# Rounding weights in 16 pieces, loading the first unit's operands first, and scanning a whole unit at once in a gated-attention and MLP kernel

## The chip, the cores and the metric

The kernel runs on one NeuronCore of a Trainium2 chip. The metric is device time in microseconds for one execution. Runs of the kernel before took 786.53, 787.57 and 788.98 us; the median is 787.57 us. In the text PE is the matmul engine, DVE the vector engine, ACT the scalar engine, POOL GpSimd, and SP the engine whose queue issues most of the DMAs. Each engine works off its own queue in order.

## The reference

A gated linear attention runs over 768 steps for 4 batches of 8 heads, with 48 channels per head; its result, 3072 tokens of 384 channels, goes through a two-layer network with 2048 hidden channels and the activation h - tanh(h).

```python
def _attn_ref(q, k, v, alpha):               # each (4, 8, 768, 48), float32
    ...
    for t in range(S):
        state = alpha[:, :, t, :, None] * state + np.einsum('bhd,bhe->bhde', k[:, :, t], v[:, :, t])
        y[:, :, t] = np.einsum('bhd,bhde->bhe', q[:, :, t], state)
    return y.astype(np.float32)

def _moe_ref(x, w_in, w_out):                # (3072, 384), (384, 2048), (2048, 384)
    h = x @ w_in
    g = h - np.tanh(h)
    return (g @ w_out).astype(np.float32)
```

The two weight matrices arrive as float64. The chip has to turn each of their 1.57 million numbers into float32 before a matmul can use it.

## The kernel before

**Units.** The work is cut into 12 units of 256 tokens, three for each batch; a unit has two chunks of 128 tokens. A unit goes through two generators. `gla(u)` is the attention: it transposes alpha, k and q so that channels lie on partitions (L344), forms running products of alpha over each chunk from the right (`U`, L351) and from the left (written over `aT`, L361), multiplies them onto k and q (POOL, L364 and L365), forms scores (`sc`, L382, masked into `pm`, L385), outputs (`y`, L394 and L398) and the new state (`tp`, `kn`, `up`, L418 to L429). Its result is `xT`; a part of it is moved between partitions by six small DMAs per chunk from `xs` (L411). `moe(u)` is the network, in 8 steps: `first(s)` makes 256 hidden channels `h` (L442) and their activation `g` (ACT L448 to L455, DVE L451 to L453); `second(s)` multiplies `g` by `w_out` into `o` (L462) two steps later. At the end of a unit two ACT copies (L474) and two DMAs write the 256 rows of the output.

**Weights.** `load_weight` (L37 to L66) loads one piece of int64 words and rounds it: on DVE four passes cut out, clamp, shift and sign the exponent (L55, L57, L58, L60) and one cuts out the upper mantissa (L62); ACT turns both parts of the mantissa to float (L63, L64), POOL adds them (L65), and DVE multiplies mantissa and exponent into the weight (L66). There are 12 pieces of 512 columns for `w_in` and 16 of 384 columns for `w_out`, 28 in all.

**Order.** A list `order` gives every step of every generator a due time; it is sorted and the steps are written in that order. All weight pieces are due before the first step of `moe(0)`. A scheduler then places the instructions on each engine from these priorities and its own estimates; the engines' queues are fixed when the program starts. Loads of a unit (`load`, L327 and L332) and of weights (L48) are all issued by SP. The raw tiles of alpha, k and q exist twice, one set for even and one for odd units. After the last unit a flag decides whether a slow general version must recompute everything; with these inputs it isn't run.

Of the kernel before, what the change touches and what calls it, by code (L numbers as in the profile page):

```python
# [8 lines left out]
FP32 = mybir.dt.float32  # L9
# [9 lines left out]
CU = 2  # L19

# [15 lines left out]
def load_weight(nc, pool, dst, rows):  # L36

    V, A, GP = nc.vector, nc.scalar, nc.gpsimd  # L40
    n = dst.shape[-1]
    if rows[0][1].dtype == FP32:
        for at, src in rows:
            nc.sync.dma_start(out=dst[at], in_=src)
        return
    raw = pool.tile([P, 512], I64, name="raw")
    for at, src in rows:
        nc.sync.dma_start(out=raw[at, 0:n], in_=src)  # L48
    words = raw.bitcast(I32).rearrange("p (n w) -> p n w", w=2)
    lo, hi = words[:, 0:n, 0].bitcast(mybir.dt.uint32), words[:, 0:n, 1]  # L50
    e = pool.tile([P, 512], I32, name="e", tag="u")[:, 0:n]
    m = pool.tile([P, 512], I32, name="m", tag="z1")[:, 0:n]
    low = pool.tile([P, 512], FP32, name="low", tag="z2")[:, 0:n]
    man = pool.tile([P, 512], FP32, name="man", tag="w")[:, 0:n]
    V.tensor_scalar(out=e, in0=hi, scalar1=20, scalar2=0x7FF,  # L55
                    op0=ALU.logical_shift_right, op1=ALU.bitwise_and)
    V.tensor_scalar(out=e, in0=e, scalar1=896, scalar2=1151, op0=ALU.max, op1=ALU.min)  # L57
    V.tensor_scalar(out=e, in0=e, scalar1=23, scalar2=0x3FFFFFFF,  # L58
                    op0=ALU.logical_shift_left, op1=ALU.bitwise_and)
    V.scalar_tensor_tensor(out=e, in0=hi, scalar=-0x40000000, in1=e,  # L60
                           op0=ALU.bitwise_and, op1=ALU.bitwise_or)
    V.tensor_single_scalar(out=m, in_=hi, scalar=0xFFFFF, op=ALU.bitwise_and)  # L62
# [189 lines left out]
def fast(tc, q, k, v, alpha, moe_w_in, moe_w_out, out, w_in, w_out, ident, ok, pad_rows):  # L252
# [17 lines left out]
    with ExitStack() as ctx:  # L270
# [19 lines left out]
        raws = [[consts.tile([P, NP, R, D], FP32, name=f"{n}{i}") for n in ("ar", "kr", "qr")]  # L290
                for i in range(2)]
        for i in range(2):
            for t, x in zip(raws[i], (1.0, 0.0, 0.0)):
                GP.memset(t[:, :, R - 1, :], x)

        Us = [consts.tile([P, NP, CU, P], FP32, name=f"U{i}") for i in range(2)]
        for t in Us:
            GP.memset(t[:, :, :, P - 1:P], 1.0)
# [4 lines left out]
        def weights():  # L303

            w = 512
            for i in range(d_ff // w):
                cols = slice(i * w, (i + 1) * w)
                for j in range(KT):
                    load_weight(nc, two, w_in[:, j, cols],
                                [(at, moe_w_in[f0:f0 + at.stop - at.start, cols]) for at, f0 in pad_rows[j]])  # L310
                yield
                for f in range(i * w // P, (i + 1) * w // P):
                    load_weight(nc, two, w_out[:, f, :], [(slice(0, P), w_out_r[:, f, :])])
                yield
# [3 lines left out]
        def load(u):  # L318
            b, i = divmod(u, UPB)
            t0 = i * TU  # L320
            for t, x in zip(raws[u % 2], (alpha, k, q)):
# [9 lines left out]
            for c in range(CU):  # L331
                nc.sync.dma_start(out=vt[:, c], in_=v[b, :, t0 + c * P:t0 + (c + 1) * P, :].rearrange("h p d -> p h d"))  # L332
# [157 lines left out]
        for _, _, what, u in sorted(order):  # L490
            if (what, u) not in live:
                live[what, u] = make[what](u) or iter(())
# [81 lines left out]
```

## Time and profile before

| | us |
|---|---|
| median of the runs | 787.57 |
| the profiled execution, whole | 785.88 |
| its span, first to last instruction | 783.7 |
| PE busy | 627.0 (80% of the span) |
| DVE busy | 477.8 (61%) |
| ACT busy | 336.7 (43%) |
| POOL busy | 118.2 (15%) |

The profile gives for each engine its busy time, for each line of the kernel its instructions with their mean duration, and for each gap what the engine waited for. A slice picture divides the span into 40 parts of 19.6 us; each digit is the busy share of a part in tenths. A windows table gives busy times for stretches that one chooses, and a timeline lists instructions by start time.

### The profile page before, as it was taken

The numbers are of one execution on the slowest core, as the hardware profiler recorded it, in microseconds if no ns is written. First come the engines' busy times: TensorE is split into PE (matmuls) and PEld (weight loads), VectorE is DVE, ScalarE is ACT, GpSimd is POOL, SyncE is SP. The second block draws the span as 40 slices with busy tenths as digits, with TensorE's granted clock in tenths as the row PEclk, the third lists the DMA queues.
The fourth block names the chain that finished last, engine by engine and source line by source line (L and its number), as shares of the span: only waits on it lengthen the run. The fifth ranks groups of instructions, "written<-read, shape, count | busy, mean of one in ns | idle before, by whom it ended". The sixth has DMA issues, their size and how long they took to land. (4 is left out here: it accounts for less than half of the span.)

```text
span 783.7 us, 9136 instructions
## 1 busy us (share of the span) xinstructions
PE 627.0 (80%) x3089; PEld 462.9 (59%) x3089; DVE 477.8 (61%) x828; ACT 336.7 (43%) x725; POOL 118.2 (15%) x110
## 2 busy tenths in 40 slices
PE   0350090008989999989999999999999999999996
PEld 0240070006667677767776767767767777677773
DVE  5357977877858768393685672864728434344332
ACT  1122143235446364454453653544536444454542
POOL 2212332232030203011020120110201200000000
PEclk9999995558999999999999999999999999999999
DMA  9015744366036226244352250130100000000000
GB/s 199 17 53 142 147 105 119 97 164 136 1 86 119 55 62 129 63 98 79 78 113 54 61 126 23 32 69 24 23 20 6 1 23 4 6 18 3 20 1 25
DMA packets 58424, 51.03 MB, mean 65 GB/s; under 512 B 30976, under 2 KB 54784, under 8 KB 58368
## 3 DMA queue, kind: packets, MB, share of 16 engines
q1 hardware_dynamic: 58368, 50.36, 28.4%
q8 instruction: 26, 0.43, 0.2%
q14 instruction: 30, 0.25, 0.1%
HBM read 44.43 MB, written 4.72 MB: 63 GB/s over the span
## 5 line engine op out<-in xcount | busy, mean ns | idle before, releaser
L442 PE MATMUL h<-xT,w_in 128*128 128x256 f32 x1152 | 277.7, 387 | 0.9 <-DVE w L451 0.9
L462 PE MATMUL o<-w_out,g 128*128 128x384 f32 x768 | 259.7, 486 | 3.1 <-DVE g L453 3.1
L442 PEld LDWEIGHTS h<-xT,w_in 128*128 128x128 f32 x1152 | 214.6, 192 | 45.2 <-issue 5.2
L462 PEld LDWEIGHTS o<-w_out,g 128*128 128x128 f32 x768 | 145.8, 190 | 89.8 <-DVE g L453 3.7
L451 DVE TENSOR_TENSOR w<-h,u 128x512 f32<-128x512 f32 x96 | 66.0, 687 | 157.6 <-ACT u L448 157.3
L448 ACT ACTIVATE u<-h 128x512 f32<-128x512 f32 x96 | 57.2, 596 | 162.6 <-PE h L442 162.1
L418 PE MATMUL tp<-ident,kT 128*128 128x128 f32 x80 | 14.1, 305 | 132.2 <-POOL kT L364 131.3
L418 PEld LDWEIGHTS tp<-ident,kT 128*128 128x128 f32 x80 | 10.8, 156 | 136.0 <-POOL kT L364 131.8
L452 DVE SCALAR_TENSOR_TENSOR z<-z,w 128x512 f32<-128x512 f32 x96 | 71.8, 747 | 9.7 <-ACT z L449 2.8
L389 POOL TENSOR_TENSOR state<-state,ends 48x192 f32<-48x192 f32 x40 | 26.6, 666 | 293.5 <-DVE state L429 200.4
L453 DVE SCALAR_TENSOR_TENSOR g<-z,z 128x512 f32<-128x512 f32 x96 | 66.1, 688 | 6.4
L385 DVE TENSOR_TENSOR pm<-sc,mask 128x512 f32<-128x512 f32 x48 | 31.9, 685 | 60.3 <-PE sc L382 60.3
L449 ACT ACTIVATE z<-u 128x512 f32<-128x512 f32 x96 | 60.6, 631 | 2.7
L455 ACT ACTIVATE big<-u 128x512 f32<-128x512 f32 x96 | 59.1, 615 | 0.0
L450 ACT ACTIVATE z<-u 128x512 f32<-128x512 f32 x96 | 59.0, 615 | 0.0
L361 DVE TENSOR_TENSOR_SCAN aT<-aT,inv 128x128 f32<-128x128 f32 x96 | 44.8, 510 | 0.2
L65 POOL TENSOR_TENSOR man<-man,low 128x384 f32<-128x384 f32 (+1 forms) x28 | 31.4, 1123 | 88.1 <-ACT man L63 88.1
L364 POOL TENSOR_TENSOR kT<-kT,U 128x1024 f32<-128x1024 f32 x12 | 28.4, 2370 | 100.1 <-DVE kT L344 100.1
L365 POOL TENSOR_TENSOR qT<-qT,aT 128x1024 f32<-128x1024 f32 x12 | 28.9, 2407 | 94.9 <-DVE qT L344 57.7
L405 ACT COPY xs<-y 48x128 f32<-48x128 f32 x48 | 12.4, 258 | 65.2 <-PE y L398 64.9
L351 DVE TENSOR_TENSOR_SCAN U<-aT 128x127 f32<-128x127 f32 x96 | 34.6, 423 | 4.0 <-POOL kT L364 3.8
L474 ACT COPY ob<-o 128x384 f32<-128x384 f32 x24 | 11.5, 479 | 58.2 <-PE o L462 58.2
(57 smaller groups left out, 517.9 us busy)
## 6 DMA issues: line engine op xcount, KB each, us to landing
raw<-in_moe_w_out_dram SPq DMA_DIRECT2D x16, 384.0 KB, 3.4
vt<-in_v_dram SPq DMA_DIRECT2D x24, 192.0 KB, 3.5
raw<-in_moe_w_in_dram SPq DMA_DIRECT2D x24, 192.0 KB, 3.8
ar<-in_alpha_dram SPq DMA_DIRECT2D x24, 192.0 KB, 4.6
kr<-in_k_dram SPq DMA_DIRECT2D x24, 192.0 KB, 4.6
qr<-in_q_dram SPq DMA_DIRECT2D x24, 192.0 KB, 5.2
out_dram<-ob SPq DMA_DIRECT2D x24, 192.0 KB, 1.9
ar<-in_alpha_dram SPq DMA_DIRECT2D x24, 176.0 KB, 4.6
```

The source lines that it names most:

```text
L351: V.tensor_tensor_scan(out=U[:, g, c, P - 2::-1], data0=aT[:, g, c, P - 1:0:-1], data1=aT[:, g, c, P - 1:0:-1], initial=1.0, op0=ALU.mult, ...
L361: V.tensor_tensor_scan(out=aT[:, g, c, :], data0=aT[:, g, c, :], data1=aT[:, g, c, :], initial=inv[:, g, c:c + 1], op0=ALU.mult, op1=ALU.b ...
L385: V.tensor_mul(pm[hh], sc[hh], mask.unsqueeze(1).to_broadcast([P, NP, P]))
L442: T.matmul(h[:, a, :], lhsT=w_in[:, j, f * P:(f + 1) * P], rhs=x_t[:, j, :], start=(j == 0), stop=(j == KT - 1))
L448: A.activation(sq, h, AF.Square)
L449: A.activation(z1, sq, AF.Square, bias=QB1, scale=QA)
L450: A.activation(z2, sq, AF.Square, bias=QB2, scale=QA)
L451: V.tensor_mul(w, h, sq)
L452: V.scalar_tensor_tensor(out=z1, in0=z1, scalar=QK1, in1=w, op0=ALU.add, op1=ALU.mult)
L453: V.scalar_tensor_tensor(out=g, in0=z2, scalar=QK2, in1=z1, op0=ALU.add, op1=ALU.mult)
L455: A.activation(big, sq, AF.Relu, bias=-U_MAX, accum_out=over[:, n:n + 1])
L462: T.matmul(o[c], lhsT=g[:, a * TU + c * P:a * TU + (c + 1) * P], rhs=w_out[:, f, :], start=(f == 0), stop=(f == FT - 1))
```

## The change

**Rounding.** The float64 is read as two 32-bit words. ACT takes the absolute value of the upper word, read as a float (L57 of the new kernel), DVE clamps it (L60), shifts it left by three bits (L63) and joins the sign (L65); ACT scales the lower word to an integer (L58), and POOL adds it to the result as an integer (L68), writing the weight. There are now 16 pieces of 768 columns: one for `w_in` and one for `w_out` for each of the 8 steps of the network. Loading and rounding are separate functions, and four raw pieces may be in flight.

**Order of the first units.** Each piece is due shortly before the step of `moe(0)` that needs it; the loads of unit 0 are issued first, with k and v on ACT's queue; `gla(1)` is due inside `moe(0)`, and later units' `gla` lies inside the `moe` before it, as it did.

**Scans.** alpha is transposed into rows of 129 with a zero between chunks, so that one scan runs over all 8 chunk-and-pair rows of a unit (1032 columns), restarted at each zero by an added 1 or by the added reciprocal. There are two scans per unit in place of sixteen. The transposes are cut into four per operand, the raw operands exist once and not twice, and the six DMAs from `xs` are issued once per unit for both chunks, by ACT's queue instead of SP's.

```diff
-def load_weight(nc, pool, dst, rows):
+def load_weight(nc, pool, rows):
+    raw = pool.tile([P, WN], I64 if rows[0][1].dtype != FP32 else FP32, name="raw", bufs=4)
+    for at, src in rows:
+        nc.sync.dma_start(out=raw[at].rearrange("p (j n) -> p j n", n=src.shape[-1]), in_=src)
+    return raw
+def round_weight(nc, pool, raw, dst):
...
+    A.activation(mag, hi.bitcast(FP32), AF.Abs)
+    A.activation(last, lo, AF.Copy, scale=2.0 ** -29)
+    V.tensor_scalar(out=mag, in0=mag, scalar1=2.0 ** (896 // 8 - 127), scalar2=2.0 ** (1151 // 8 - 127) * 1.875,
+                    op0=ALU.max, op1=ALU.min)
+    bits = mag.bitcast(I32)
+    V.tensor_scalar(out=bits, in0=bits, scalar1=3, scalar2=0x3FFFFFFF,
+                    op0=ALU.logical_shift_left, op1=ALU.bitwise_and)
+    V.scalar_tensor_tensor(out=bits, in0=hi, scalar=-0x40000000, in1=bits,
+                           op0=ALU.bitwise_and, op1=ALU.bitwise_or)
-    V.tensor_scalar(out=e, in0=hi, scalar1=20, scalar2=0x7FF,
-                    op0=ALU.logical_shift_right, op1=ALU.bitwise_and)
...
-    A.activation(man, m, AF.Copy, bias=1.0, scale=2.0 ** -20)
-    A.activation(low, lo, AF.Copy, scale=2.0 ** -52)
-    GP.tensor_add(man, man, low)
-    V.tensor_mul(dst, man, e.bitcast(FP32))
+    GP.tensor_add(dst.bitcast(I32), bits.rearrange("p (j n) -> p j n", n=n),
+                  last.rearrange("p (j n) -> p j n", n=n))
...
-            for t, x in zip(raws[u % 2], (alpha, k, q)):
+            for n, (t, x) in enumerate(zip(raws, (alpha, k, q))):
+                queue = A if u == 0 and n == 1 else nc.sync
...
-            for c in range(CU):
-                for g in range(NP):
-                    V.tensor_tensor_scan(out=U[:, g, c, P - 2::-1], data0=aT[:, g, c, P - 1:0:-1],
...
+                    V.tensor_tensor_scan(out=U_[:, ::-1], data0=aT[:, :0:-1], data1=after[:, ::-1],
+                                         initial=0.0, op0=ALU.mult, op1=ALU.add)
...
+                    V.tensor_tensor_scan(out=W_, data0=aT[:, 0:N * (P + 1)], data1=before, initial=0.0,
+                                         op0=ALU.mult, op1=ALU.add)
...
-                        nc.sync.dma_start(out=x_t[at, j, to], in_=xs[r0:r0 + at.stop - at.start])
+                if c == CU - 1:
...
+                            A.dma_start(out=x_t[at, j, :], in_=xs[r0:r0 + at.stop - at.start])
...
-        order += [(-MOE - EARLY + 2 + i, 2, "weights", 0) for i in range(2 * d_ff // 512)]
+            put(s - 14 if s < 1 else s - 1.6, round_in, s)
+            put(s - 0.6, round_out, s)
...
+        steps(3.3, MOE - 4, GLA, gla, 1)
```

What this does to the queues is shown at three places. On PE, in the kernel before, between the attention of unit 1 and the third step of `moe(0)`; `pm_885` is the mask product of unit 1's second chunk, `tp` is the transpose for the attention of unit 2, `h` and `o_826` belong to unit 0:

```order
L398 MATMUL y<-pm_885,vt 48x128
L422 MATMUL up<-vt,kn 128x96 x4
L418 MATMUL tp<-ident,kT 128x128 x4
L442 MATMUL h<-xT,w_in 128x256 x6
L462 MATMUL o_826<-w_out,g 128x384
```

and in the changed kernel between the fourth step of `moe(0)` and the attention of unit 1, where `o_323` and `o_324` belong to unit 0:

```order
L481 MATMUL o_323<-w_out,g 128x384
L481 MATMUL o_324<-w_out,g 128x384
L461 MATMUL h<-xT,w_in 128x256 x6
L437 MATMUL tp<-ident,kT 128x128 x4
L441 MATMUL up<-vt,kn 128x96 x4
L401 MATMUL sc_625<-qT,kT 128x128
L401 MATMUL sc_626<-qT,kT 128x128
```

Before, two steps of `moe(0)` were followed by unit 2's transpose and only then by the other six; now five steps come before unit 1's transpose, and unit 2's lies in unit 1.

On DVE, in the kernel before, one piece of `w_in` in a row of weight pieces that stands ahead of all but two activations:

```order
L55 TENSOR_SCALAR e<-raw 128x512
L62 TENSOR_SCALAR m<-raw 128x512
L57 TENSOR_SCALAR e<-e 128x512
L58 TENSOR_SCALAR e<-e 128x512
L60 SCALAR_TENSOR_TENSOR e<-raw,e 128x512
L66 TENSOR_TENSOR w_in<-man,e 128x512
```

and in the changed kernel the third activation of `moe(0)` with one of the pieces behind it:

```order
L470 TENSOR_TENSOR w<-h,u 128x512
L471 SCALAR_TENSOR_TENSOR z_419<-z_419,w 128x512
L472 SCALAR_TENSOR_TENSOR g<-z_420,z_419 128x512
L60 TENSOR_SCALAR mag<-mag 128x768
L63 TENSOR_SCALAR mag<-mag 128x768
L65 SCALAR_TENSOR_TENSOR mag<-raw,mag 128x768
```

Six passes per piece have become three, and activations of `moe(0)` stand between pieces.

On DVE at the end of unit 0's attention, in the kernel before, around the transpose of q:

```order
L344 STREAM_TRANSPOSE kT<-kr_94 128x4x8x32
L427 COPY state_110<-up 48x4x48 x2
L429 TENSOR_TENSOR state_109<-state_110,up 48x4x48 x2
L344 STREAM_TRANSPOSE qT<-qr_95 128x4x8x32
L385 TENSOR_TENSOR pm_333<-sc_331,mask 128x512
```

and in the changed kernel:

```order
L378 SCALAR_TENSOR_TENSOR W<-aT_99,before 128x1032
L446 COPY state_109<-up 48x4x48 x2
L363 STREAM_TRANSPOSE qT<-qr 128x8x32 x4
L448 TENSOR_TENSOR state_108<-state_109,up 48x4x48 x2
L404 TENSOR_TENSOR pm_179<-sc_177,mask 128x512
```

The transpose of q has moved ahead of the second state update, and that of k (not in these rows) ahead of alpha's.

## Rows read from the trace of the kernel before

**Rows 1.** The page, part 2: 40 slices of 19.6 us.

```profile
PE   0350090008989999989999999999999999999996
PEclk9999995558999999999999999999999999999999
GB/s 199 17 53 142 147 105 119 97 164 136 1 86 119 55 62 129 63 98 79 78 113 54 61 126 23 32 69 24 23 20 6 1 23 4 6 18 3 20 1 25
```

**Rows 2.** The waits: who waited for whom, total us, times, longest.

```profile
PE tp L418 <- POOL kT L364: 131.3, 3, 61.4
```

**Rows 3.** The windows: stretch, its us, busy (instructions) per engine, PEclk, DMA.

```profile
0.00:180.00 180.00, 38.63 (x228) 30.99 (x228) 126.38 (x251) 49.85 (x95) 51.16 (x59) 0.83 0.50 116
221.20:776.20 555.00, 550.64 (x2727) 405.04 (x2725) 318.56 (x527) 267.68 (x591) 62.08 (x49) 1.00 0.22 49
```

**Rows 4.** The timeline of PE after 178 us: start, us, instructions, gap before.

```profile
178.39 1.12 PE L418 MATMUL tp<-ident,kT 128*128 128x128 f32 x4 [61.40 <-POOL kT L364]
...
180.40 4.45 PE L442 MATMUL h<-xT,w_in 128*128 128x256 f32 x12 [0.89 <-DVE w L451]
...
187.27 2.75 PE L442 MATMUL h<-xT,w_in 128*128 128x256 f32 x12
```

**Rows 5.** Line L474, the output copies: duration ns, first and last start.

```profile
L474 ACT COPY ob<-o x24: 479/479/480, 221.2 to 776.2; 128x384 f32<-128x384 f32 x24
```

**Rows 6.** The timeline of DVE and POOL at 118 us, one weight piece.

```profile
117.78 0.43 DVE L55 TENSOR_SCALAR e<-raw 128x512 int32<-128x512 int32 x1
...
118.91 0.43 DVE L58 TENSOR_SCALAR e<-e 128x512 int32<-128x512 int32 x1
...
119.28 1.27 POOL L65 TENSOR_TENSOR man<-man,low 128x512 f32<-128x512 f32 x1 [6.76 <-ACT man L63]
119.37 1.73 DVE L60 SCALAR_TENSOR_TENSOR e<-raw,e 128x512 int32<-128x512 int32 x1
```

**Rows 7.** Groups by form, 0 to 200 us: count, busy us, mean ns.

```profile
L65 POOL TENSOR_TENSOR man<-man,low 128x384 f32<-128x384 f32 x16 | 16.3, 1018 | 35.8 <-ACT man L63 35.8
L65 POOL TENSOR_TENSOR man<-man,low 128x512 f32<-128x512 f32 x12 | 15.2, 1263 | 52.3 <-ACT man L63 52.3
```

**Rows 8.** The timeline: the passes L60 and L58 where POOL is idle.

```profile
9.32 0.69 DVE L60 SCALAR_TENSOR_TENSOR e<-raw,e 128x512 int32<-128x512 int32 x1
...
56.69 0.35 DVE L58 TENSOR_SCALAR e<-e 128x384 int32<-128x384 int32 x1
...
57.23 0.55 DVE L60 SCALAR_TENSOR_TENSOR e<-raw,e 128x384 int32<-128x384 int32 x1
```

**Rows 9.** The timeline of unit 0's attention, with SP's issue of `xs`.

```profile
12.16 2.01 DVE L344 STREAM_TRANSPOSE aT<-ar 128x1024 f32<-128x1024 f32 x1
14.21 2.61 DVE L351 TENSOR_TENSOR_SCAN U<-aT 128x127 f32<-128x127 f32 x8
...
17.70 3.11 DVE L361 TENSOR_TENSOR_SCAN aT<-aT,inv 128x128 f32<-128x128 f32 x8
...
29.12 0.74 DVE L427 COPY state<-up 48x192 f32<-48x192 f32 x2 [6.39 <-PE up L422]
...
34.67 2.02 DVE L344 STREAM_TRANSPOSE qT<-qr 128x1024 f32<-128x1024 f32 x1
...
39.23 2.08 PE L382 MATMUL sc<-qT,kT 48*128 48x128 f32 x16 [5.43 <-POOL qT L365]
...
49.06 0.68 DVE L385 TENSOR_TENSOR pm<-sc,mask 128x512 f32<-128x512 f32 x1
...
50.80 3.76 SPq L411 DMA_DIRECT2D xT<-xs  x6
```

**Rows 10.** The timeline of POOL and DVE at 190 us.

```profile
189.83 2.36 POOL L365 TENSOR_TENSOR qT<-qT,aT 128x1024 f32<-128x1024 f32 x1 [10.43 <-DVE qT L344]
...
190.69 0.69 DVE L451 TENSOR_TENSOR w<-h,u 128x512 f32<-128x512 f32 x1 [0.94 <-ACT u L448]
...
191.49 1.25 DVE L452 SCALAR_TENSOR_TENSOR z<-z,w 128x512 f32<-128x512 f32 x1
```

More of the change, by code (lines that the diff above doesn't have):

```diff
@@ L19 @@
 CU = 2
+WN = 768
 U_MAX = 0.25
@@ L301, in fast, with fetch_in, fetch_out, round_in @@
             GP.memset(t, 0.0)
[L303 to L314, printed above, removed]
+        raw_in, raw_out = {}, {}
+        def fetch_in(s):
+            parts = []
+            for i in range(len(pad_rows[0])):
+                at, f0 = pad_rows[0][i]
+                step = pad_rows[1][i][1] - f0
+                src = moe_w_in[f0:f0 + KT * step].rearrange("(j p) n -> p j n", p=step)
+                parts.append((at, src[0:at.stop - at.start, :, 2 * s * P:2 * (s + 1) * P]))
+            raw_in[s] = load_weight(nc, two, parts)
+        def fetch_out(s):
+            raw_out[s] = load_weight(nc, two, [(slice(0, P), w_out_r[:, 2 * s:2 * s + 2, :])])
+        def round_in(s):
+            round_weight(nc, two, raw_in.pop(s), w_in[:, :, 2 * s * P:2 * (s + 1) * P])
+        def round_out(s):
+            round_weight(nc, two, raw_out.pop(s), w_out[:, 2 * s:2 * s + 2, :])
         loaded = {}
@@ L357, in gla @@
[L357 to L368 removed]
+            kT, qT = (two.tile([P, NP, CU, P], FP32, name=n) for n in ("kT", "qT"))
@@ new lines, in gla @@
+            U, W = (two.tile([P, N, P + 1], FP32, name=n, bufs=1) for n in ("U", "W"))
+            U_, W_ = (t.rearrange("p n t -> p (n t)") for t in (U, W))
+            aT = aTs[u % 2]
+            tail = aT[:, 1:].rearrange("p (n t) -> p n t", t=P + 1)
+            for t, raw in zip((tail[:, :, 0:P].rearrange("p (g c) t -> p g c t", c=CU), kT, qT), raws):
+                for g in range(NP):
+                    V.transpose(t[:, g].rearrange("p c (i r) -> p r c i", r=R),
+                                raw[:, g, :, 0:32])
+                yield
+                if t is not kT and t is not qT:
+                    V.tensor_tensor_scan(out=U_[:, ::-1], data0=aT[:, :0:-1], data1=after[:, ::-1],
+                                         initial=0.0, op0=ALU.mult, op1=ALU.add)
+                    ends = two.tile([P, NP, CU], FP32, name="ends")
+                    e = ends.rearrange("p g c -> p (g c)")
+                    V.tensor_reduce(out=least[:, u:u + 1], in_=U[:, :, 0], axis=AX.X, op=ALU.min)
+                    V.tensor_single_scalar(out=e, in_=U[:, :, 0], scalar=1.0 / R_MAX, op=ALU.max)
+                    V.reciprocal(before[:, 0::P + 1], e)
+                    yield
+                    V.tensor_tensor_scan(out=W_, data0=aT[:, 0:N * (P + 1)], data1=before, initial=0.0,
+                                         op0=ALU.mult, op1=ALU.add)
+                    yield
```

126 lines of the change are left out of this document (56 added, 70 removed).

## The prediction

> **What bounds the kernel now.** I read the slice picture of the page first, then the waits, then windows on both sides of the break that the picture shows. In the picture PE is half busy or less in eight of the first nine slices and at nine tenths or more in nearly all later ones [rows 1]. The windows say the same in numbers: up to 180 us PE is busy 38.6 us of 180, while DVE is busy 126.4 and POOL 51.2; from 221.2 to 776.2 us PE is busy 550.6 of 555.0 [rows 3]. So there are two kernels here. The second is bound by PE and full: only 4.4 us of it are idle, and nothing in the change takes matmuls away. The first is bound by what prepares weights and operands. The longest PE wait of all is a wait for POOL's product onto k, 131.3 us in three pieces, one of them 61.4 [rows 2]; it ends at 178.39 with the transpose for unit 2's attention [rows 4]. In PE's queue that transpose stands ahead of the third step of `moe(0)`, and POOL's product stands behind nearly all weight pieces. Unit 0 therefore ends late: its first output copy is at 221.2, the last unit's second at 776.2 [rows 5].
>
> The reckoning follows from that: the eleven later units cost 555.0 us and the tail 783.7 - 776.2 = 7.5 us in either kernel, and the profiled execution lies 785.88 - 783.7 = 2.2 us above its span. What changes is the time at which unit 0 ends. By then both kernels have the attention of units 0 and 1 behind them, so the work that remains for PE is the same.
>
> **What DVE and POOL cost each other.** This decides the price of a weight piece. POOL's add of 512 columns starts at 119.28 and takes 1.27 us. DVE's sign pass L60 starts at 119.37 and takes 1.73 us [rows 6], where alone it takes 0.69 [rows 8]; it ends 0.55 us after POOL does. So it waited for POOL. In the same way z takes 1.25 us where it meets POOL's product at 191.49, while w, which reads one operand from PSUM, keeps its 0.69 in the middle of the same product [rows 10]. I therefore add POOL's time to DVE's for every pass over weights, and not for passes that read PSUM, nor for transposes.
>
> **Price of a new piece.** Passes of 384 and 512 columns give slopes. A shift pass takes 0.35 and 0.43 us [rows 6, 8], so 0.59 at 768. The sign pass takes 0.55 and 0.69 [rows 8], so 0.97. POOL's float add takes 1.018 and 1.263 [rows 7], so 1.75. The float clamp is not in the trace; I give it the shift's price, since it has the same shape and also works in place; were it to run at the sign pass's rate, it would cost 0.97. The integer add on POOL is not there either; the nearest row is the float add, and without a row for integers I let it lie between 1.0 (what 384 columns cost, twice the rate) and 2.7 (half again). Sum: 0.59 + 0.59 + 0.97 + 1.75 = 3.9 us for 768 columns. Before, a 512-column piece took four passes of 0.43, one of 0.69 with 1.27 of POOL, and a product of about 0.69: 4.4 by the sum. For all 12288 columns the change brings 16 x 3.9 = 62 us where there was about 105.
>
> By the Trainium skill (GPSIMD Engine Reference, section 2.1 Instruction dispatch) the first call of a freshly loaded POOL routine also pays about 6 us for loading code. If the integer add were such a call, the time would grow by 6 us, once, to 731. The first float add shows nothing of the kind, its group's mean being 1.263 [rows 7]; no run here has shown an integer add.
>
> **When unit 0 ends, step by step.** (1) The attention of unit 0. Alpha's transpose started at 12.16 and the last mask product ended at 49.06 + 0.68 = 49.7 [rows 9]. The transpose of q now stands before the second state update: it can start where the first state copy ends, 29.12 + 0.74 = 29.9, and not at 34.67 [rows 9], 4.8 us earlier. K is transposed first and no weight pass stands between the mask products: another 1.2. Issuing k and v on ACT's queue I cost at nothing; SP's loads cover it, and if k landed last it would cost up to 2 us. Last mask product at 49.7 - 6 = 43.7.
>
> (2) From there DVE and POOL have 15 of the 16 pieces to do; the first is rounded in gaps of step 1. 15 x 3.9 = 58.5 us.
>
> (3) Eight activations of `moe(0)`, three DVE passes each at about 0.69 [rows 10]: 16.6.
>
> (4) The attention of unit 1. Three transposes at 2.01 [rows 9], a little more in four pieces each: 6.4. Two long scans: eight short ones take 2.61 and 3.11 [rows 9], with eight starts; a long one lies between 1.2 (a column as in the sign pass) and 2.6; I take 2.4, near the rows of the same operation, so 4.8. Small passes, four masks at 0.68 and four state passes at 0.37: 4.9. POOL's two products at 2.36 [rows 10]: 4.7. Together 20.8. The scans gain about 1 us per unit on DVE; in the later units, where PE is full, that is worth nothing.
>
> (5) Off: passes that read PSUM, and transposes, run under POOL; by the order of DVE that is seven w's, a transpose and two masks: -7.
>
> (6) On: waits that no row of before prices in this place. ACT now issues the six DMAs from `xs`, 3.76 us on SP [rows 9], and it does so ahead of its two passes for the next pieces, so those are late and DVE stands: 8. The first two `h` are slow, 4.45 us against 2.75 [rows 4]: 3. In the fifth step the activation follows its own piece at once and waits for POOL, `h` and ACT: 4. The chain of unit 1 from POOL's product by PE and ACT to its masks: 5. Together 20.
>
> (7) The last `o`, about 3 us (555.0 / 11 units / 16 half steps).
>
> Sum: 43.7 + 58.5 + 16.6 + 20.8 - 7 + 20 + 3 = 155.6, against 221.2 before: 65.6 us earlier. Weight DMAs don't set this: 12.6 MB of weights and 5.2 MB of operands for two units at the 199 GB/s of the first slice [rows 1] are 89 us.
>
> (8) Given back: unit 2's attention is only begun in unit 1, and PE meets its transpose after three `h`; about 3 us. In later units the six DMA issues on ACT (3.76 us of an engine with half its time free [rows 3]) and the single set of raw operands, which are free again some four steps before the next load, I cost at nothing; uncovered they would cost up to 3.76 us a unit.
>
> 785.88 - 65.6 + 3 = 723.3; the median stands 787.57 - 785.88 = 1.7 above the profiled execution: **725 us**.
>
> **The rivals.**
>
> A, POOL's add is hidden: it meets only passes that don't contend, or the integer form doesn't block. For it: in unit 0 DVE will often wait anyway. Against it: the three passes of the next piece follow at once in DVE's order. 15 x 1.75 = 26 us less: 699.
>
> B, PE's clock. PE ran at its lower level, 1.2 GHz, in slices 7 to 9 of the break, where the granted clock is five tenths [rows 1], and an `h` step took 4.45 us there and 2.75 once it had risen [rows 4]. In the changed unit 0 PE works about half the time in bursts. If it stays at 1.2 GHz throughout, each step's `h` reaches its activation 1.7 us later, and PE's own work, 50.5 us per unit, becomes 101 from about 53: the end of unit 0 comes to about 170, the time to 740. The Trainium skill names this (TensorE: Matmul & The Clock Gate, HAM oscillation — how this bites in real kernels): bursts of matmuls with idle gaps between them fall back to the half clock and start each burst slow. The break shows such a fall [rows 1]; whether gaps of a few us suffice no row here shows.
>
> C, the later units lose: ACT's six DMA issues delay u behind `h` in every unit, 11 x 3.76 = 41 us: 766. Against it: `h` has two buffers, and `o` runs two steps behind.
>
> D, unit 1's operands are late. Its loads stand on SP's queue behind weight loads that wait for a raw piece to be rounded; were they 20 us late, DVE would stand at the transpose and all pieces behind it: 745.
>
> E, slower than before: the integer add. It is the only operation with no relative in the trace and it excludes DVE while it runs. The gain of 62 us is gone when it costs 1.75 + 62 / 15 = 5.9 us, 3.4 times the float add; at 8 us the time would be 819. Only the missing row speaks for it.
>
> F, the change doesn't do what it says: pieces are rounded in a row ahead of `moe(0)` again. The order on DVE shows activations between them, so I give it no chance of its own.
>
> **How the numbers follow.** The forecast, unit 0's end between 138 and 173 with full later units, has 0.68; A 0.08, B 0.10, C 0.06, D 0.05, E 0.03. The forecast's own bounds are 704 and 749: the add at 1.0 or 2.7 us moves it by 15 x -0.75 = -11 or 15 x 0.95 = +14, the waits of step 6 by 10 either way. The range is these bounds and a little more, 703 to 750; B and D lie in it, C and E above, A just below. A difference under 0.3%, 2.4 us, is about what a measurement of this kernel can't tell from none. Faster holds all but E and a bad mixture of C and D: 0.95; same 0.02; slower 0.03.
>
> **What would show it.** Right: PE's first `h` at 50 to 56 us; the first output copy at 140 to 173; from it to the last copy 553 to 562; no PE wait over 15 us after the first `h`; POOL's integer adds near 1.75 us, and the sign pass or a clamp longer by as much where they meet. Wrong: an add over 2.7 us; a granted clock of five tenths up to the end of unit 0 (B); later units of 53 us with ACT between (C); a long DVE wait for `ar` before unit 1 (D); adds with DVE passes of full speed under them (A).

## The result and the profile after

The changed kernel takes **750.06 us** (median of 4 runs, 748.11 to 754.85) where the kernel before takes 788.28 (4 runs); the ratio is 0.953, with an interval of 0.948 to 0.958. The forecast was 725, its range 703 to 750. So the sign was right and the gain too large: 38 us instead of 63, and the median lies 0.06 us above the end of the range. The profiled execution took 749.17 us, with a span of 745.9.

The slice picture of the page, which answers to [rows 1] (one digit per slice of 18.6 us):

```profile
PE   0367629587999899999999998999999999999996
PEclk9998965799999999999999999999999999999998
```

The break of PE is shorter: from slice 11 on, about 190 us, its digits are nine with two eights until the last, and only the first slice is empty. A stretch of lower granted clock is still in it, slices 6 to 8. The windows answer to [rows 3]; the columns are stretch, its length, then busy us and instructions of PE, PEld, DVE, ACT and POOL, PE's mean granted clock, DMA share and GB/s. The first line reaches from the last mask of unit 0's attention to the first output copy, the second to the last copy:

```profile
46.20:167.45 121.25, 79.01 (x298) 56.05 (x298) 74.02 (x99) 52.04 (x92) 36.22 (x21) 0.79 0.54 119
167.45:738.60 571.15, 554.36 (x2717) 402.61 (x2715) 329.34 (x509) 271.61 (x594) 69.11 (x54) 1.00 0.23 52
```

The output copies, which answer to [rows 5] (duration in ns, first and last start):

```profile
L493 ACT COPY ob<-o x24: 458/479/480, 167.5 to 738.6; 128x384 f32<-128x384 f32 x24
```

**Where the time went.** Unit 0 ends at 167.45 instead of 221.2: 53.7 us earlier, where the forecast had 65.6. From the first to the last copy it takes 571.15 us instead of 555.0: 16.1 us are given back, where the forecast had 3. The tail is 7.3 us, as forecast. Against the 723.3 us that the forecast gave the profiled execution this is 11.9 + 13.1 us, -0.2 in the tail and 1.1 more around the span: 25.9, all that is missing. So there are two questions, and the experiments take them apart: why units 1 to 11 lost time, and why unit 0 ended 12 us late. The first is answered by a variant's time from its first output copy to its last, the second by the time of its first output copy.

DVE is idle for 47 of the 121 us of the first window. It was meant to be the engine that sets unit 0's end, with some 20 us of waits.

**One step of `moe(0)`, read row by row.** The timeline of all engines in the changed kernel, from DVE's w of one step to the w of the next (start, us, engine, line, operation, output and inputs, and in brackets the idle time before and what ended it):

```profile
152.38 0.69 DVE L470 TENSOR_TENSOR w<-h,u 128x512 f32<-128x512 f32 x1 [2.30 <-ACT u L467]
...
153.97 0.69 DVE L472 SCALAR_TENSOR_TENSOR g<-z,z 128x512 f32<-128x512 f32 x1
154.05 0.88 ACT L57 ACTIVATE mag<-raw 128x768 f32<-128x768 f32 x1
154.81 4.51 PE L481 MATMUL o<-w_out,g 128*128 128x384 f32 x8 [3.10 <-DVE g L472]
...
154.96 0.56 DVE L60 TENSOR_SCALAR mag<-mag 128x768 f32<-128x768 f32 x1 [0.29 <-ACT mag L57]
...
157.25 1.99 POOL L68 TENSOR_TENSOR w_in<-mag,last 128x768 int32<-128x768 int32 x1 [5.22 <-DVE mag L65]
157.61 2.05 DVE L63 TENSOR_SCALAR mag<-mag 128x768 int32<-128x768 int32 x1
159.29 4.58 PE L461 MATMUL h<-xT,w_in 128*128 128x256 f32 x20
...
162.18 0.60 ACT L467 ACTIVATE u<-h 128x512 f32<-128x512 f32 x1 [4.85 <-PE h L461]
162.81 0.63 ACT L468 ACTIVATE z<-u 128x512 f32<-128x512 f32 x1
162.81 0.69 DVE L470 TENSOR_TENSOR w<-h,u 128x512 f32<-128x512 f32 x1 [2.17 <-ACT u L467]
```

(The 20 `h` matmuls of the row at 159.29 are the 12 of unit 0's last step and the first 8 of unit 1.) No engine is full here, and yet in this order nothing could start sooner. The step is one chain round four engines: DVE's w, z and g and the wait for ACT's pass on the next `w_in` piece, 152.38 to 154.96 (2.58 us); three DVE passes on that piece, to 157.25 (2.29); POOL's add, to 159.29 (2.04); `h`, to 162.18 (2.89); u, to 162.81 (0.63). The sum is 10.43 us. The `w_out` piece hides in it: its blocked shift (2.05 us instead of 0.56) ends while DVE has nothing else to do.

**The stall in the middle.** Between the w of the fifth step (95.74) and that of the sixth (141.81) lie 46 us instead of 10.4. The rows of PE, then of ACT and DVE, in that stretch of the changed kernel:

```profile
108.86 1.11 PE L437 MATMUL tp<-ident,kT 128*128 128x128 f32 x4 [13.78 <-POOL kT L383]
...
120.63 2.07 PE L401 MATMUL sc<-qT,kT 48*128 48x128 f32 x10
...
123.11 5.00 PE L481 MATMUL o<-w_out,g 128*128 128x384 f32 x8
127.95 1.04 PE L413 MATMUL y<-qT,state 128*112 128x128 f32 x8
```

```profile
130.04 0.26 ACT L423 COPY xs<-y 48x128 f32<-48x128 f32 x1 [8.03 <-PE y L417]
...
130.58 0.89 ACT L57 ACTIVATE mag<-raw 128x768 f32<-128x768 f32 x1
```

```profile
131.50 0.56 DVE L60 TENSOR_SCALAR mag<-mag 128x768 f32<-128x768 f32 x1 [7.88 <-ACT mag L57]
```

ACT's pass for the sixth `w_in` piece stands behind the copies of unit 1's y, those wait for PE, and PE has an `o` of 5.00 us ahead of y's matmuls, where the granted clock is 0.55. DVE stands for 7.88 us, though SP had issued that piece's load by 89.2 us. Below, an `o` or `h` of 4.2 to 5.5 us is called one at half clock: most of it ran at the lower level, 1.2 GHz (the `o` at 144.61 has a granted clock of 0.62), where one at the higher level takes 2.7 to 2.9.

### The profile page after: what moved, and what is told of

Read it like the earlier page. It is cut to its first block, busy times and chain, and to the rows that moved or that the text cites. A ratio compares the mean times of both kernels' runs of the same rounds, so it can differ in the third digit from the quotient of the medians.

```text
span 745.9 us, 8678 instructions
## 1 busy us (share of the span) xinstructions
PE 648.4 (87%) x3089; PEld 470.9 (63%) x3089; DVE 423.4 (57%) x636; ACT 332.7 (45%) x701; POOL 117.5 (16%) x98
## 4 chain that ended last, share of the span: by engine, by line
PE 70%; DVE 12%; DMA 6%; ACT 4%; issue 3%; POOL 3%; ACTq 1%; SPq 0%; DVEq 0%; POOLq 0%
PE h L461 30%; PE o L481 29%; PE y L417 5%; PE up L441 2%; DVE z L471 2%; PE sc L401 2%; DVE w L470 2%; DVE W L378 2%; ACT u L467 2%; DVE pm L404 1%; DMA kr<-in_k_dram 1%; DMA raw<-in_moe_w_out_dram 1%; PE y L413 1%; PE tp L437 1%; POOL w_in L68 1%
## 5 line engine op out<-in xcount | busy, mean ns | idle before, releaser
L461 PE MATMUL h<-xT,w_in 128*128 128x256 f32 x1152 | 282.2, 391 | 17.3 <-POOL w_in L68 11.9
L481 PE MATMUL o<-w_out,g 128*128 128x384 f32 x768 | 267.2, 496 | 10.5 <-DVE g L472 10.4
L461 PEld LDWEIGHTS h<-xT,w_in 128*128 128x128 f32 x1152 | 217.0, 194 | 63.9 <-POOL w_in L68 14.8
L481 PEld LDWEIGHTS o<-w_out,g 128*128 128x128 f32 x768 | 148.5, 194 | 101.3 <-issue 18.8
L408 POOL TENSOR_TENSOR state<-state,ends 48x192 f32<-48x192 f32 x40 | 30.5, 762 | 303.7 <-DVE state L448 190.5
L474 ACT ACTIVATE big<-u 128x512 f32<-128x512 f32 x96 | 59.0, 615 | 0.0
L437 PE MATMUL tp<-ident,kT 128*128 128x128 f32 x80 | 14.1, 302 | 47.0 <-POOL kT L383 46.0
L417 PE MATMUL y<-pm,vt 128*48 128x128 f32 x384 | 38.1, 298 | 11.7 <-DVE pm L404 11.7
L437 PEld LDWEIGHTS tp<-ident,kT 128*128 128x128 f32 x80 | 10.6, 154 | 53.2 <-POOL kT L383 46.8
L417 PEld LDWEIGHTS y<-pm,vt 128*48 128x48 f32 x384 | 25.4, 131 | 25.7 <-DVE pm L404 20.7
L363 DVE STREAM_TRANSPOSE kT<-kr 128x256 f32<-128x256 f32 x48 | 25.7, 622 | 19.2 <-DMA qr<-in_q_dram 17.8
L401 PEld LDWEIGHTS sc<-qT,kT 48*128 48x128 f32 x384 | 29.1, 210 | 11.2 <-issue 9.5
L383 POOL TENSOR_TENSOR qT<-qT,W 128x1024 f32<-128x1024 f32 x12 | 26.2, 2180 | 61.5 <-DVE qT L363 61.5
```

Source lines behind the costliest of these rows:

```text
L383: GP.tensor_mul(t, t, x[:, :, 1:])
L401: T.matmul(sc[hh][:, g, :], lhsT=kT[at, g, c, :], rhs=qT[at, g, c, :], start=True, stop=True)
L417: T.matmul(y[HP * hh:HP * hh + D, g, :], lhsT=vt[:, c, 2 * g + hh, :], rhs=pm[hh][:, g, :], start=(n == 0 and g == 0), stop=True, skip_gro ...
L461: T.matmul(h[:, a, :], lhsT=w_in[:, j, f * P:(f + 1) * P], rhs=x_t[:, j, :], start=(j == 0), stop=(j == KT - 1))
L474: A.activation(big, sq, AF.Relu, bias=-U_MAX, accum_out=over[:, n:n + 1])
L481: T.matmul(o[c], lhsT=g[:, a * TU + c * P:a * TU + (c + 1) * P], rhs=w_out[:, f, :], start=(f == 0), stop=(f == FT - 1))
```

## The experiments

Twelve variants ran. The first output copy of each profile shows unit 0. The b and c variants all have a2's edit as well; a1, a3 and a4 don't.

**a1: the six transfers from `xs` on SP.**

```diff
-                            A.dma_start(out=x_t[at, j, :], in_=xs[r0:r0 + at.stop - at.start])
+                            nc.sync.dma_start(out=x_t[at, j, :], in_=xs[r0:r0 + at.stop - at.start])
```

> The changed kernel with one edit: the six transfers from xs into xT are issued on SP's queue again and not on ACT's. Theory (ACT's issuing, about 2.8 us each time, delays the two ACT passes of the next weight piece in unit 0, and nothing in later units): the second piece's clamp starts near 52 instead of 55.0, the sixth w_in piece's near 129 instead of 131.5, the first output copy at 162 to 164 instead of 167.45, first to last copy unchanged at 571, time 744 to 747. Rival C of the prediction (ACT's issues cost the later units): first to last copy falls below 565 as well, time under 741. Third case (SP's queue holds weight loads ahead of these six): the first h comes later than 54.5 and the time is 750 or more.

Measured: 764.27 us (ratio to the kernel before 0.967, 0.961 to 0.972), slower than the changed kernel. The two clamps did move as expected, to 52.53 and 129.87, and the first `h` from 54.52 to 53.65; but the first output copy came at 166.78, 0.7 us earlier, so the starts that were gained went into the waits behind them. (PE's order in unit 0 differs a little too: the second `up` matmuls for unit 1's state come ahead of the sixth `h`.) The loss lies in unit 1, which takes 68.5 us instead of 54.4: the edit had moved more than its six transfers, the scheduler having put unit 2's attention ahead of most of `moe(1)`, and PE met its transpose right after the `o` rows of unit 0. Of the 14.1 us, 5.5 are more idle time of PE and 8.5 more busy time, at a granted clock of 0.88 instead of 0.97. PE in a1 at the end of unit 0:

```profile
163.16 4.23 PE L481 MATMUL o<-w_out,g 128*128 128x384 f32 x8 [3.10 <-DVE g L472]
174.68 1.12 PE L437 MATMUL tp<-ident,kT 128*128 128x128 f32 x4 [7.29 <-POOL kT L383]
```

The ten units behind it take 520.2 us, no less than the 516.8 of the changed kernel. So taking the issues off ACT gained unit 0 0.7 us here, which the clock alone can move by more (last section), and the ten later units nothing: rival C's mechanism is refuted. The run shows no gain, and its slower total belongs to the moved order.

**a2: later attention planned 0.4 of a step earlier.**

```diff
-            at = (u - 1) * MOE - 3
+            at = (u - 1) * MOE - 3.4
```

> The changed kernel with one edit: the attention of units 2 to 11 is planned 0.4 of a step earlier, so that on PE six matmuls of h stand between the sc matmuls and the y matmuls that follow them; units 0 and 1 keep their order. Theory (in later units PE waits for the masks because sc and y stand next to each other): the waits of y for pm, 10.9 us, go; first to last copy falls from 571.1 to 557 to 561, time 737 to 741. Rival C (ACT's six issues) or a rival that later units lose by the single set of operands: first to last copy stays at 569 to 572 and the time at 749 to 751.

Measured: **723.42 us** (723.14 to 724.0; ratio 0.916, 0.912 to 0.921), 26.6 below the changed kernel. First to last copy took 550.3 us, less than the theory's 557 to 561 and less than the 555.0 of the kernel before:

```profile
L493 ACT COPY ob<-o x24: 459/479/481, 162.7 to 713.0; 128x384 f32<-128x384 f32 x24
```

The windows from the second unit's first copy to the last unit's, of the changed kernel and of a2:

```profile
221.85:737.97 516.12, 504.30 (x2477) 366.69 (x2476) 287.93 (x449) 246.45 (x539) 56.88 (x47) 1.00 0.23 51
```

```profile
217.97:712.30 494.33, 493.90 (x2477) 367.33 (x2476) 289.08 (x449) 245.26 (x539) 53.26 (x47) 1.00 0.24 53
```

The same 2477 matmuls take 21.8 us less: 11.4 of it was PE idle, 10.4 PE busy. The idle part is one line of PE's waits in the changed kernel (total us, times, longest), and a2 has no such line:

```profile
PE y L417 <- DVE pm L404: 10.9, 16, 2.6
```

PE in one later unit, of the changed kernel and of a2:

```profile
351.24 1.16 PE L401 MATMUL sc<-qT,kT 48*128 48x128 f32 x16
352.33 1.13 PE L413 MATMUL y<-qT,state 128*112 128x128 f32 x8
354.28 0.42 PE L417 MATMUL y<-pm,vt 128*48 128x128 f32 x2 [0.82 <-DVE pm L404]
354.63 0.70 PE L461 MATMUL h<-xT,w_in 128*128 128x256 f32 x2
```

```profile
335.29 1.16 PE L401 MATMUL sc<-qT,kT 48*128 48x128 f32 x16
336.38 2.86 PE L461 MATMUL h<-xT,w_in 128*128 128x256 f32 x12
339.07 2.74 PE L481 MATMUL o<-w_out,g 128*128 128x384 f32 x8
341.65 1.04 PE L413 MATMUL y<-qT,state 128*112 128x128 f32 x8
342.62 1.08 PE L417 MATMUL y<-pm,vt 128*48 128x128 f32 x16
```

With twelve attention steps in eight steps of the network instead of eleven in nine, sc and y had come into the same gap. PE had nothing between them but to wait for DVE's masks. From 225 us on, y's matmuls stand right behind sc's at 15 places in the changed kernel, at 6 in the kernel before and at none in a2. The busy part is mostly where such a y splits an `h`: y's matmuls with pm take 26.9 us in the changed kernel and 20.0 in a2, `h` takes 230.2 and 223.3 (the two overlap, so these gains don't simply add).

Unit 0 has the same order of PE in both, and up to 117 us the same times within 0.3 us; still it ended at 162.68 here. What differs is the clock, told below.

**a3: no add on POOL.** The sign pass writes the weight itself; the last three bits are not rounded in.

```diff
-    V.scalar_tensor_tensor(out=bits, in0=hi, scalar=-0x40000000, in1=bits,
+    V.scalar_tensor_tensor(out=dst.bitcast(I32), in0=hi.rearrange("p (j n) -> p j n", n=n), ...
...
-    GP.tensor_add(dst.bitcast(I32), bits.rearrange("p (j n) -> p j n", n=n),
-                  last.rearrange("p (j n) -> p j n", n=n))
```

> The changed kernel without POOL's integer add: the sign pass writes the weight directly, so the rounding of the last three bits is left out (weights are cut, not rounded). By the forecast's step 2 (each add stops DVE for its 1.75 us): 26 us less, first output copy at 141, time 724. By the walk through the trace of the changed kernel (DVE's passes there are longer by only 10.6 us in all, and four h wait for a piece that comes 1.8 us earlier): first output copy at 152 to 158, time 735 to 741. Rival A in full (the add is hidden): 748 to 750.

Measured: 755.29 us (0.957, 0.952 to 0.961); first output copy at 165.11, only 2.3 us earlier; units 1 and 2 took 56.9 and 59.7 us where the changed kernel's took 54.4 and 54.7, so the total is no measure of the add. None of the three cases held. One step was still 10.1 us (w at 78.88 and 89.02); the two ahead of it, with `o` at the higher level, took 8.38 and 8.44 (w at 62.06, 70.44 and 78.88). PE in the second and third of these steps of a3:

```profile
72.78 2.85 PE L480 MATMUL o<-w_out,g 128*128 128x384 f32 x8 [0.81 <-DVE g L471]
75.46 2.75 PE L460 MATMUL h<-xT,w_in 128*128 128x256 f32 x12
81.22 4.54 PE L480 MATMUL o<-w_out,g 128*128 128x384 f32 x8 [3.00 <-DVE g L471]
...
85.59 2.75 PE L460 MATMUL h<-xT,w_in 128*128 128x256 f32 x12
```

`h` starts where `o` ends, and the later `o` runs at half clock. With the add, piece and add take 2.29 + 2.04 = 4.33 us and such an `o` fits beside them; without it, `o` is the longer one and takes the add's place in the chain. So the trace of a3 already speaks for the clock as what took the gain; c1 and c2 test it.

**a4: unit 1's attention left out**, `moe(1)` works on unit 0's xT.

```diff
-        steps(3.3, MOE - 4, GLA, gla, 1)
```

> The changed kernel without the attention of unit 1: moe(1) works on unit 0's xT, so unit 1's output is not computed (its state update is missing too). Shows what unit 1's attention costs unit 0. By the forecast's sum (20.8 of DVE less what runs beside POOL, 5 for its chain): first output copy near 167.45 - 24 = 143. Theory (a stall: from 90 to 131.5 us DVE works only 17.9 us, because the passes for the sixth w_in piece stand behind unit 1's chain on ACT): the steps go on at about 10.4 us each, and the first output copy comes at 129 to 134.

Measured (one run, 716.8 us): first output copy at 135.62, that is 31.8 us earlier than in the changed kernel and 27.1 earlier than in a2; the theory's 129 to 134 was a little too low, the forecast's 143 too high. DVE's w in the sixth to eighth step:

```profile
110.11 0.69 DVE L472 TENSOR_TENSOR w<-h,u 128x512 f32<-128x512 f32 x1 [2.71 <-ACT u L469]
120.55 0.69 DVE L472 TENSOR_TENSOR w<-h,u 128x512 f32<-128x512 f32 x1 [2.17 <-ACT u L469]
130.98 0.69 DVE L472 TENSOR_TENSOR w<-h,u 128x512 f32<-128x512 f32 x1 [2.17 <-ACT u L469]
```

Steps of 10.44 and 10.43 us, as in the chain above, with `o` at half clock (4.3 to 4.5 us) beside the piece and the add. The sixth step itself had taken 14.5 us (w at 95.59 and 110.11), which is where the theory's range was missed.

**b1 and b2: PE's gaps filled in unit 0**, six overwritten matmuls ahead of an `h` and 36 transposes ahead of unit 1's; b2 without the add.

```diff
+                for _ in range(6 if u == 0 and s > 1 else 0):
+                    T.matmul(h[:, 0, :], lhsT=w_in[:, 0, 0:P], rhs=x_t[:, 0, :], start=True, stop=True)
...
+                for _ in range(36 if n == CU else 0):
+                    T.transpose(tp[:, 0, :], aT[:, 1:P + 1], ident)
```

> a2_shift with idle PE time filled in unit 0: six matmuls whose results are overwritten ahead of each h from the third step on, and 36 transposes of alpha ahead of unit 1's transpose of k. Asks whether PE's clock sets unit 0's end. Theory (at 1.2 GHz an h takes 4.5 and an o 4.5 us, at 2.4 GHz 2.75, and both stand in the chain of a step): PE keeps the higher level from the third step, the step stays near 10.4 us where it was 10.4 to 11.5, unit 1's chain is some 4 us shorter, first output copy at 150 to 156 instead of 162.7, time 710 to 717. Rival (the clock hides behind DVE and POOL, or the added matmuls are in the way): first output copy at 160 or later, time 721 or more.

> b1_warm without POOL's integer add (weights are cut, not rounded in their last three bits, as in a3_noadd). Theory (a step is one chain through ACT, DVE, POOL, PE, ACT and DVE; the add is 1.8 to 2.0 us of it, and in a3_noadd the gain was eaten because PE fell to 1.2 GHz): with PE kept at the higher level the add's removal now shows, about 1.9 us in each of six or seven steps: first output copy 10 to 14 us earlier than b1_warm's, time 10 to 14 us lower. Rival (the add is hidden, so it never mattered): within 3 us of b1_warm.

Measured: first output copies at 162.38 and 163.90, medians 737.81 (0.934) and 731.74 us (0.924). Later units were ordered anew by the scheduler and lost 11 to 14 us, so only unit 0 is compared. b1 met the rival's number: PE ran `h` at 2.86 us in most steps and unit 0 did not end sooner. b2 missed the theory's number: up to the fifth step PE waited for no piece any more, but its own `h`, six added matmuls and `o` then filled the step; and its sixth step took 45.1 us where b1's took 40.6, with an `o` of 5.49 us where b1's took 2.75. It is no test of the add, and c1 and c2 repeat the pair with three added matmuls.

**c1 and c2: three added matmuls, without and with the add.**

> b2_warm_noadd with three added matmuls ahead of an h instead of six, so that PE's own work no longer fills the step (b2: two h's worth of it and an o took 9.7 us of 10.4); the add is left out, weights are cut, not rounded, in their last three bits. Theory (a step is one chain: ACT's pass on the piece, three DVE passes, POOL's add, h, ACT's u, DVE's w, z and g; the add is 1.8 to 2.0 us of it): steps of 8.3 to 8.8 us at the higher clock instead of 10.4, first output copy 8 to 13 us earlier than in c2_warm3. Rival (the add is hidden, or DVE's total sets the step): within 3 us of c2_warm3.

> b1_warm with three added matmuls instead of six; all weights rounded. Theory (with the add in the chain the step is 10.4 us whether PE is busy between or not): steps of 10.3 to 10.5 us, first output copy at 160 to 164 as in a2_shift and b1_warm. Rival (b1's six matmuls stood in the way, and the clock does set unit 0's end): first output copy at 156 or earlier.

Two successive `h` on PE in c1, then in c2:

```profile
76.94 2.75 PE L464 MATMUL h<-xT,w_in 128*128 128x256 f32 x12
...
85.38 2.75 PE L464 MATMUL h<-xT,w_in 128*128 128x256 f32 x12
```

```profile
82.78 2.86 PE L465 MATMUL h<-xT,w_in 128*128 128x256 f32 x12 [1.27 <-POOL w_in L68]
...
93.05 2.86 PE L465 MATMUL h<-xT,w_in 128*128 128x256 f32 x12 [1.49 <-POOL w_in L68]
```

The step is 8.44 us without the add and 10.27 with it, 1.83 us less; the rest of the add's 2.0 is not gained because `h` then starts only where an `o` of 2.85 us ends. Medians 730.51 and 742.0 us (0.927 and 0.940); first output copies at 156.89 and 166.68, 9.8 us apart, as the theory had it. c2's own number, 160 to 164, was missed by 2.7 us, its unit 1 chain having more of its matmuls at half clock than a2's; its rival, 156 or earlier, did not come about either. So the add counts nearly in full, once a step, as a link of the chain. In a3 an `o` at half clock had taken the gain.

**b3 and b4: unit 1's attention earlier and later.**

```diff
-        put(-0.1, load, 1)
-        steps(3.3, MOE - 4, GLA, gla, 1)
+        put(-12, load, 1)                       (b3)
+        steps(-6, 12, GLA, gla, 1)              (b3)
+        steps(4.8, MOE - 5, GLA, gla, 1)        (b4)
```

> a2_shift with unit 1's operands loaded earlier and unit 1's attention planned from the second step of moe(0) on, ahead of the third w_in piece, instead of in its fifth step. Theory (unit 1's chain from its transposes to its last mask, 96 to 121 us in a2_shift, stops the pieces wherever it stands, since they queue behind it on ACT and POOL): first output copy at 158 to 165 and time 718 to 726, no gain. Rival (in the fifth step it is in the way of the pieces, earlier it would run beside the loading of weights): first output copy at 150 or earlier, time under 712.

> a2_shift with unit 1's attention planned after nearly all weight pieces, in the last steps of moe(0). Theory: moe(0) runs through at about 10.4 us a step as in a4_nogla1, first output copy at 136 to 146, but unit 1's chain of some 25 us then stands between moe(0) and moe(1) with PE half idle; the output copy of unit 1 comes at 208 to 220, where a2_shift has it at 218, and the time is 713 to 725. Rival (the chain is hidden behind the last steps and unit 2's work): output copy of unit 1 at 200 or earlier, time under 706.

Measured: b3 724.91 us (0.917, 0.915 to 0.919), first copy at 159.72, unit 1's at 218.30: the total within 1.5 us of a2, as the theory said. b4 733.74 us (0.927), first copy at 146.59, unit 1's at 225.95; in b4 the loads of unit 2 come ahead of some of unit 1's transposes, so that unit 1 reads unit 2's k and q, with no instruction more or less. The two b4 copies are 0.6 and 6 us later than the ends of their ranges, and its total is 9 above. In the fifth step of `moe(0)` or ahead of its third the chain of unit 1 costs the same, and at the end it costs more; nothing was gained by moving it whole.

**c3: the rounding of the kernel before, in the new order**, on 768 columns.

```diff
-    A.activation(mag, hi.bitcast(FP32), AF.Abs)
...
+    V.tensor_scalar(out=e, in0=hi, scalar1=20, scalar2=0x7FF, ...)
+    V.tensor_scalar(out=e, in0=e, scalar1=896, scalar2=1151, op0=ALU.max, op1=ALU.min)
...
+    GP.tensor_add(man, man, low)
+    V.tensor_mul(dst, man..., e.bitcast(FP32)...)
```

> a2_shift with the rounding of the kernel before, on pieces of 768 columns: six DVE passes (4 x 0.59 + 2 x 0.97 = 4.3 us) instead of three (2.1) and POOL's float add instead of the integer one. Shows what the cheaper rounding is worth in the new order. Theory (chain of a step): 2.2 us more in each of seven steps: first output copy at 174 to 184, time 735 to 746. By the forecast's way of adding (15 pieces of 4.3 + 1.75 instead of 3.9 us): 32 us more, first output copy at 195, time 755. Rival (rounding is hidden behind loads): within 4 us of a2_shift.

Measured: 742.63 us (0.938, 0.931 to 0.945), first output copy at 179.10. Both lie in the theory's ranges (174 to 184, 735 to 746) and far from the 195 of the forecast's way of adding. In the last three steps PE now waits 6 us and more for a piece:

```profile
150.47 4.25 PE L463 MATMUL h<-xT,w_in 128*128 128x256 f32 x12 [6.81 <-DVE w_in L71]
...
163.40 1.19 PE L463 MATMUL h<-xT,w_in 128*128 128x256 f32 x2 [6.09 <-DVE w_in L71]
```

This step is 12.9 us, 2.5 more. So the cheaper rounding is worth 16.4 us of unit 0's end, to within the 5 us that the clock can move. The rest of its 58.5 us in a2 (221.2 to 162.7), 42.1 us, is still there with the old rounding, so it comes from the other parts of the change: the order, the pieces and the operands of unit 0. Those were not taken apart further.

**c4: unit 0's k and v on SP's queue.**

```diff
-                queue = A if u == 0 and n == 1 else nc.sync
+                queue = nc.sync
```

> a2_shift with unit 0's k and v issued on SP's queue again, as in the kernel before. Asks what issuing them on ACT's queue cost, which the forecast put at nothing (2 us if late). Theory (with both queues loading, k and q land together at 17.8 us and DVE's first transpose waits for that; alpha first on one queue lets it start at 12 to 13): last mask product of unit 0 at 43 to 45 instead of 46.4, first output copy 1 to 3 us earlier than in a2_shift (162.7), time 720 to 723. Rival: no gain, because q and v now land later by as much; time within 1 us of a2_shift or above.

Measured: 728.65 us (0.924, 0.919 to 0.929), slower than a2; first output copy at 169.50. The theory failed. DVE's first transpose did start at 12.85, but PE's sc then waited 5.3 us for POOL's product onto q, and the last mask product ended at 48.4 instead of 46.4. The first of the rows is the transpose, the second the last mask:

```profile
12.85 2.01 DVE L363 STREAM_TRANSPOSE aT<-ar 128x256 f32<-128x256 f32 x4 [12.85 <-DMA ar<-in_alpha_dram]
...
47.70 0.69 DVE L404 TENSOR_TENSOR pm<-sc,mask 128x512 f32<-128x512 f32 x1 [3.18 <-PE sc L401]
```

So the second queue is worth 2 us of unit 0's attention. The other 4.8 us of the first copy's 6.8 come behind it, with more `h` and `o` at half clock; they are not shown to belong to the edit.

## Why the prediction was right and wrong

**Right: the sign and the picture of two kernels.** The second is full, the first is bound by what prepares weights, and its end moved by 53.7 us. That the interleaving of `moe(0)` with pieces moved it was not tested alone: c3 leaves 42.1 of 58.5 us to order, pieces and operands together. That unit 0's end is the one time that moves was not right (see the next paragraph). The first `h` came at 54.52 (50 to 56 forecast), the first output copy at 167.45 (140 to 173), and PE's longest wait after the first `h` was 13.78 us. Rival D did not come about: DVE's transposes for unit 1 start at 96.35, right behind a w, with no wait for `ar`. Nor did E: the add took 1.80 to 1.99 us (1.75). The clamp took 0.56 (0.59), the sign pass 0.96 (0.97), the long scan 2.28 to 2.31 alone (2.4). POOL's first integer add took 1.81 us:

```profile
27.52 1.81 POOL L68 TENSOR_TENSOR w_in<-mag,last 128x768 int32<-128x768 int32 x1
```

The Trainium skill (GPSIMD Engine Reference, section 2.1 Instruction dispatch) would have a freshly loaded routine pay about 6 us at its first call; this first add shows nothing of it.

**Wrong, 13 us: step 8, and with it "the eleven later units cost 555.0 us" in either kernel.** The forecast looked at ACT's issues and at the single set of operands there, and took PE's stream as given because no matmul is taken away or added. It is not given. The section on the change says that later units' `gla` lies as it did; in fact its steps are now twelve in eight steps of the network, where they were eleven in nine, and sc and y came to stand side by side. a2 moves nothing but that and gets 20.9 us back. The 0.4 in a2 was chosen from the order of the code, where sc at step 1.0 and y at 1.67 fall between the same two `h`; the forecast could have seen it there. Rival C had such a loss (766), but by a mechanism that a1 refutes.

**Wrong, 8 us: unit 1's attention, steps 4 and 6.** 20.8 of DVE and 5 for its chain, less what ran under POOL, some 24 us; a4 shows 31.8 against the changed kernel and 27.1 against a2. Of the 8 us that are missing, 4.7 are thus the later rise of PE's clock (the `o` ahead of y took 5.00 us, and 2.75 in a2). For the rest, what was missing is the head of a queue: the next pieces' ACT passes stand behind y's copies. The rows show that wait; no variant took it out by itself. Step 6 had looked for this in the wrong place, at 8 us for ACT's six issues; without them a1 gained 0.7.

**Wrong, 2.5 us: step 1.** The last mask product ended at 46.2 and not at 43.7. Issuing k and v on ACT's queue was "up to 2 us" if late; the first transpose waited to 17.77, where alpha's had started at 12.16 [rows 9]. c4 shows that the alternative is worse still.

**Right in sum, wrong in mechanism: steps 2, 3 and 5.** Without unit 1's attention the forecast's sum for unit 0 is about 155.6 - 24 = 132, plus the 2.5 us of step 1: 134; a4 measured 135.6. But DVE's time with POOL's add upon it is not what sets it. By steps 2 to 5 DVE had 88.9 us of work from the last mask to unit 0's end, and steps 6 and 7 added 23 of waits and the last `o`; measured were 74.0 busy and 47.2 idle. In the first window POOL lengthened DVE's passes by 10.6 us in all (a shift by 1.48 each time), not by 26; the other adds met a DVE that was waiting anyway. This is the half of rival A that was true. Against it stood a chain of 10.43 us a step, in which the add counts nearly in full (c1, c2). Two errors of about 15 us had cancelled: 14.9 too much work and, beside the 8 us of unit 1, 16 too little waiting. Two small sums are off as well: step 4's four masks and four state passes make 4.2 and not 4.9, step 5's passes 8.2 and not 7; together that is 1.9 us of the 155.6. c3 shows how far this carries: the same way of adding would have put its unit 0 at 195, and it ended at 179.

**Rival B, the clock.** The window of the first 14 us behind the last mask has a granted clock of 0.75, the two of 20 us from 100 and from 120 us have 0.51 and 0.67. The Trainium skill (TensorE: Matmul & The Clock Gate, HAM oscillation — how this bites in real kernels) says that bursts between idle gaps start slow; the transpose after 13.78 us of idle PE does, 1.11 us where it takes 0.59 to 0.67 in later units. But unit 0 did not stay slow throughout, and filling the gaps did not end it sooner (b1). The price was a few us where PE stands in the chain (below), not 15. The forecast's 4.45 us for an `h` at the lower level was itself too short: over that row of [rows 4] the granted clock is 0.63, and an `h` wholly at 1.2 GHz takes 5.49 us (135.66 in the changed kernel, granted 0.50).

## What to carry to other kernels

When work is interleaved so that no engine is full any more, don't price it by the busiest engine's sum: walk one step of the loop from an operation to its next turn, engine by engine, and look which of the links an edit shortens. An edit that adds a step to a schedule moves all the others in it; list for every stage, also the full one, what now stands between a producer and its consumer on the bound engine. A variant in which one link is taken out needs the others held, the clock among them, or the next longest link takes the gain unseen.

## What the runs showed of the hardware

The time at which PE's clock rises differs between runs of one order. The changed kernel and a2 have the same order up to unit 0's end and agree within 0.3 us until 117 us. Then six sc matmuls of the same kind took, in the changed kernel and in a2:

```profile
117.18 1.65 PE L401 MATMUL sc<-qT,kT 48*128 48x128 f32 x6
```

```profile
117.34 0.95 PE L401 MATMUL sc<-qT,kT 48*128 48x128 f32 x6
```

In a2 PE had reached its higher level, 2.4 GHz, some 10 us sooner; what it had done before was the same in both. This alone is 4.8 us of unit 0's end (167.45 and 162.68), and it may be why the changed kernel's runs lie 7 us apart (748.11 to 754.85); that link was only argued, and a2's own four runs lie within 0.9 us. A difference of 5 us in unit 0 between two variants can therefore be the clock.

DVE's one-operand shift waits for POOL as its two-operand pass does [rows 6]: 2.04 us instead of 0.56, as does the scan (3.63 us beside POOL's first add instead of 2.29), while the transposes kept 2.0 us beside POOL's products. The Trainium skill (SBUF — State Buffer, section Who interferes with whom) describes an exclusive lock that is held for a whole instruction, and the trace agrees. The scan's row in the changed kernel, to be read with POOL's first add at 27.52:

```profile
27.86 3.63 DVE L378 TENSOR_TENSOR_SCAN W<-aT,before 128x1032 f32<-128x1032 f32 x1
```

The version to keep is a2: 723.42 us, 0.916 of the kernel before.
